# A decode kernel on one core: the last section of TensorE in another order, with products of zeros in its waits

## The chip, the cores and the metric

The kernel runs on one core of a Trainium2 chip. The metric is the device time of one execution in microseconds (us); lower is better. Every execution is recorded with three things: its time, its span (from the first to the last instruction of the core) and the mean clock that TensorE was granted, as a share of full speed. A full trace, with every instruction and transfer, is kept for one execution of each run. Nearly all runs below are of the state "fast"; a run with a single execution ("a look") has the state "unknown", and its span is then compared with the spans of fast executions.

## The reference, cut to what matters

One decoding step of four sequences: cached attention with 16 query heads on 8 key/value heads of 8192 positions, an output projection, and a small MLP that gates it.

```python
# x: (4, 1, 448); k_cache, v_cache: (4, 8, 8192, 256), bf16
xn = _layernorm(x)
q = (xn @ wq) ...                                  # 16 heads of 256
scores = einsum("bhqd,bhkd->bhqk", q, k) * 256 ** -0.5
o = einsum("bhqk,bhkd->bhqd", softmax(scores), v)
s = o.reshape(4, 1, 4096) @ wo                     # wo: (4096, 448)
g = silu(_B_ref(xn, w1, w2, w3, w4))               # MLP, short
return x + s * g
```

There are 32 pairs of sequence and key/value head. Each has a key tile and a value tile of 4 MB, so 268 MB come from memory, once.

## The kernel before

One queue (SP) streams key and value tiles in turn. TensorE turns the keys (transposes), multiplies them with the queries, and multiplies the values of two pairs earlier with the exponentials. The last section, `finish()`, runs after the loop: the value products of the last two pairs, and the output projection. The last value tile comes in four pieces, and behind it come three late pieces of `wo`, so that only little work is left after the last landing.

```python
PIECES = (0, 32, 48, 56, NCH)       # pieces of the last value tile
LATE = ((0, 1), (2,), (3,))         # heads of wo that are loaded last
NWARM = 18                          # products of zeros before the loop
# ... cut ...
# SP queue, at its end
load_v(NH - 2)
load_v(NH - 1)                      # four pieces: dvl0 to dvl3
for i, hs in enumerate(LATE):       # three pieces: dwl0 to dwl2
    load_wo(hs[0], hs[-1] + 1, "dwl%d" % i)
# ... cut ...
# TensorE
def f_tr(dst, width, slot=0):       # "turned products": fp32, 2 columns
    for dh in range(NHALF):
        for i in range(CP):
            ins = pe.matmul(dst(dh)[:, 0:width], po[:, slot, i*DH+dh:(i+1)*DH:NHALF],
                            sel[:, i, 0:width], start=(i == 0), stop=(i == CP - 1))
    return ins

def f_st(h):
    take(pe, "a_exp")
    pe.matmul(psm[:, P+REP:P+2*REP], ones_f[:, :], rowsum[:, h % 2, :], start=True, stop=True)
    if h < NH - 1:
        take(pe, "v_po")
    ins = f_tr(ot_dst, REP)
    if h == NH - 1:
        take(pe, "v_po")
        ins = f_tr(lambda dh: ot_dst(dh, 1), REP, 1)
    ins.then_inc(S["p_m3"], 1)

def finish():
    f_bc(h)
    take(pe, "dwo", 16)
    pe.wait_ge(S["g_f"], 1)
    f_ou(range(NLATE, HQ - 3 * REP))        # 12 output products
    take(pe, "v_po")
    take(pe, "dv%d" % ((h - 1) % 2), 16)    # next-to-last value tile
    f_pv(h - 1, 0, NCH)                     # its 32 value products
    f_st(h)                                 # sum, 8 + 8 turned products
    take(pe, "dvl0", 16)
    pb = PIECES[NPIECE - ND]
    f_pv(h, 0, PIECES[1], pb, vl)           # piece one
    take(pe, "v_ot")
    f_ou(range(HQ - 3 * REP, HQ - REP)).then_inc(S["p_ou"], 1)
    # ... cut: pieces two to four, then:
    take(pe, "dwl0", 16)
    f_o(LATE[0])
    # ... cut ...
    for i in range(1, len(LATE)):
        take(pe, "dwl%d" % i, 16)
        ins = f_o(LATE[i], i == len(LATE) - 1)   # the very last: 8 products
    ins.then_inc(S["p_o"], 1)
```

After the last product DVE does two small steps (times the gate, plus x) and the result is stored.

## Time and profile before

| | before |
|---|---|
| time, median of 3 executions | 658.86 us (658.5 to 659.02) |
| the execution of the trace | time **660.08 us**, span 658.0 us |
| DMA rate over the span | 424 GB/s |

From the page of the kernel before: the span, the busy times, three rows of the 40 slices (each digit the tenths of a slice), and the transfer queue.

```profile
span 658.0 us, 22911 instructions
PE 555.3 (84%) x9959; PEld 475.0 (72%) x9959; DVE 276.3 (42%) x593; ACT 256.1 (39%) x364; POOL 13.4 (2%) x77
...
PEclk9797999897899888789987978998788898877996
DMA  8999999999999999999999999999999999999995
...
q1 hardware_dynamic: 12336, 278.99, 99.0%
```

The DMA row stands at 9 to the end: the kernel is bound by its stream of 279 MB. TensorE's 84% lies under it. Only what stands behind the stream's end can be shortened by work on TensorE, so the end must be read closely.

The timeline of the end of the kernel before. Columns: start in us, duration of the group, engine, line, operation, output<-inputs and shapes, number of instructions, and in brackets the idle time before it.

```profile
636.95 0.75 PE L674 MATMUL pst<-wo_sb,OT 128*32 128x448 bf16 x12
640.29 3.58 PE L642 MATMUL psv<-vb,pT 128*4 128x512 bf16 x32 [2.59 <-PEq L244]
643.81 0.59 PE L628 MATMUL psm<-rowsum,ones_f 128*128 128x2 f32 x2
644.26 3.55 PE L616 MATMUL psm<-sel,po 128*128 128x2 f32 x16
647.74 1.88 PE L642 MATMUL psv<-kn,pT 128*4 128x512 bf16 x16
...
653.31 0.56 PE L694 MATMUL pst<-pT,kn 128*128 128x32 bf16 x16
653.79 0.38 PE L684 MATMUL pst<-wo_sb,OT 128*32 128x112 bf16 x16
654.33 0.61 PE L684 MATMUL pst<-wo_sb,OT 128*32 128x112 bf16 x32 [0.16 <-PEq L244]
```

The landings are read from the transfer records of the same trace: next-to-last value tile 640.2 us, pieces of the last one 645.1, 647.6, 648.8 and 650.1, late pieces of wo 651.3, 651.8 and **652.37**. The last product ended at 654.94, so it was 2.58 us late. I call this distance, from the last landing to the end of the last product, the *lateness*.

The windows view of the same end. Columns: stretch and its length, then busy time of TensorE's products, weight loads, DVE, ACT and POOL (instructions in brackets), granted clock, share of DMA busy, GB/s.

```profile
635.30:638.70 3.40, 1.46 (x21) 0.60 (x15) 1.28 (x4) 0.70 (x4) 0.00 (x0) 1.00 1.01 434
638.80:642.20 3.40, 1.91 (x20) 0.69 (x24) 0.00 (x0) 0.00 (x0) 0.00 (x0) 0.50 0.98 419
642.20:645.60 3.40, 3.40 (x25) 2.07 (x17) 0.69 (x1) 0.00 (x0) 0.00 (x0) 0.50 0.94 392
645.60:649.00 3.40, 3.40 (x27) 2.52 (x30) 0.52 (x3) 0.00 (x0) 0.00 (x0) 0.50 1.01 403
649.00:652.40 3.40, 3.32 (x49) 1.37 (x41) 1.32 (x2) 0.00 (x0) 0.00 (x0) 0.50 0.59 218
```

After a stretch with 1.46 us of work the clock is halved, and stays so for four stretches of 3.41 us (638.79 to 652.45; the drop comes 1.09 us into the wait of 2.59 us). In the first of them TensorE is busy for 1.91 us, in the other three for 3.32 us or more. In this trace the recorded clock is always at 0.5 or 1.0, and all its changes lie multiples of 3.41 us apart. I call such a stretch of 3.41 us a *window*, and the time at which one begins its *edge*.

### The profile page before, as it was taken

The page shows a single profiled execution, that of the slowest core. Times are in us where ns is not written, and L with a number is a line of the kernel's source. Part 1 is how long each engine was busy: PE and PEld are TensorE (multiplying, and loading weights), DVE is VectorE, ACT ScalarE, POOL GpSimd, SP SyncE. Part 2 cuts the span into 40 slices and gives each one's busy share as a digit, 9 for nine tenths or more (in the row PEclk, how much of TensorE's full clock was granted, in tenths as well). Part 3 has the DMA queues.
Part 4 walks back from the last instruction along what each step waited for, and adds up shares of the span by engine and source line. Part 5 has one row for each costly group of instructions (what it writes and reads, how often), then busy time and mean ns, then how long its engine had stood idle before and what let it go on. Part 6 is the DMA issues. An engine that isn't in the chain of part 4 may idle for free. (4 is left out here: it accounts for less than half of the span.)

```text
span 658.0 us, 22911 instructions
## 1 busy us (share of the span) xinstructions
PE 555.3 (84%) x9959; PEld 475.0 (72%) x9959; DVE 276.3 (42%) x593; ACT 256.1 (39%) x364; POOL 13.4 (2%) x77
## 2 busy tenths in 40 slices
PE   1898997987888988888898878898888889888877
PEld 0487886876766887676797757778776678767755
DVE  7453554443443443344433434444343344434431
ACT  4153454442433444333444423444333344433430
POOL 2000000000000000000000000000000000000000
PEclk9797999897899888789987978998788898877996
DMA  8999999999999999999999999999999999999995
GB/s 359 439 416 422 437 426 436 430 430 432 428 436 428 434 430 438 428 432 432 428 432 430 430 432 434 430 438 428 432 430 430 432 432 428 432 438 428 436 420 225
DMA packets 12370, 279.13 MB, mean 424 GB/s; under 512 B 1221, under 2 KB 3273, under 8 KB 3785
## 3 DMA queue, kind: packets, MB, share of 16 engines
q1 hardware_dynamic: 12336, 278.99, 99.0%
q8 instruction: 7, 0.11, 0.1%
q14 instruction: 3, 0.02, 0.0%
q10 hardware_dynamic: 24, 0.01, 0.0%
HBM read 278.99 MB, written 0.00 MB: 424 GB/s over the span
## 5 line engine op out<-in xcount | busy, mean ns | idle before, releaser
L586 PE MATMUL pst<-ident_b,kn 128*128 128x128 bf16 x4096 | 346.4, 238 | 76.8 <-PEq L244 76.5
L294 ACT ACTIVATE kT<-pst 128x1024 bf16<-128x1024 bf16 x224 | 229.5, 1025 | 359.1 <-ACTq L244 358.1
L586 PEld LDWEIGHTS pst<-ident_b,kn 128*128 128x128 bf16 x4096 | 274.8, 108 | 82.4 <-issue 81.9
L292 DVE COPY kT<-pst 128x1024 bf16<-128x1024 bf16 x288 | 197.5, 691 | 263.3 <-DVEq L244 263.3
L598 PE MATMUL psc<-qc,kT 128*128 128x2 bf16 x4096 | 178.8, 164 | 2.4 <-issue 2.4
L598 PEld LDWEIGHTS psc<-qc,kT 128*128 128x128 bf16 x4096 | 157.9, 98 | 31.1 <-issue 30.8
L642 PE MATMUL psv<-vb,pT 128*4 128x512 bf16 x1056 | 87.3, 386 | 2.6 <-PEq L244 2.6
L616 PE MATMUL psm<-sel,po 128*128 128x2 f32 x272 | 38.2, 263 | 0.0
L616 PEld LDWEIGHTS psm<-sel,po 128*128 128x128 f32 x272 | 36.2, 204 | 0.0
L642 PEld LDWEIGHTS psv<-vb,pT 128*4 128x4 bf16 x1056 | 22.0, 83 | 18.7 <-issue 4.7
L452 DVE TENSOR_REDUCE rmax<-psc 128x2 f32<-128x128 f32 x32 | 9.3, 292 | 48.1 <-DVEq L244 48.1
L470 DVE COPY po<-psv 128x512 f32<-128x512 f32 x34 | 23.5, 692 | 7.8 <-DVEq L244 7.1
L457 DVE TENSOR_REDUCE gmax<-psm 2x1 f32<-2x128 f32 x32 | 8.9, 279 | 34.7 <-DVEq L244 34.7
L316 ACT ACTIVATE pT<-psc,negb 128x64 bf16<-128x64 f32 x66 | 20.7, 333 | 5.4 <-ACTq L244 5.4
L610 PEld LDWEIGHTS psm<-diag,ones_f 2*128 2x128 f32 x66 | 13.5, 253 | 6.4 <-issue 5.2
L279 POOL COPY qc<-qT 128x4 bf16<-128x4 bf16 x32 | 5.9, 186 | 586.6 <-DVEq L469 569.1
L610 PE MATMUL psm<-diag,ones_f 2*128 2x2 f32 x66 | 16.2, 313 | 1.1 <-PEq L244 0.9
L316 ACT ACTIVATION_READ_ACCUMULATOR pT<-psc,negb 128x1 f32 x66 | 13.6, 206 | 0.0
L606 PEld LDWEIGHTS psm<-ident_f,rmax 128*2 128x2 f32 x32 | 2.6, 80 | 14.0 <-issue 14.0
L628 PE MATMUL psm<-rowsum,ones_f 128*128 128x2 f32 x66 | 12.2, 254 | 0.0
L534 PE MATMUL pst<-ident_b,xn_b 4*128 4x4 bf16 x14 | 0.6, 161 | 13.6 <-DVE xn_b L365 8.9
L628 PEld LDWEIGHTS psm<-rowsum,ones_f 128*128 128x128 f32 x66 | 10.0, 192 | 0.9 <-issue 0.9
(97 smaller groups left out, 105.3 us busy)
## 6 DMA issues: line engine op xcount, KB each, us to landing
kn<-in_A_k_cache_dram SPq DMA_DIRECT2D x32, 4096.0 KB, 25.7
vb<-in_A_v_cache_dram SPq DMA_DIRECT2D x31, 4096.0 KB, 30.9
vb<-in_A_wq_dram SPq DMA_DIRECT2D x1, 3584.0 KB, 11.4
vb<-in_B_w_dram SPq DMA_DIRECT2D x2, 1568.0 KB, 16.3
wo_sb<-in_A_wo_dram SPq DMA_DIRECT2D x1, 2688.0 KB, 44.1
kn<-in_A_v_cache_dram SPq DMA_DIRECT2D x1, 2048.0 KB, 24.8
kn<-in_A_v_cache_dram SPq DMA_DIRECT2D x1, 1024.0 KB, 26.9
kn<-in_A_v_cache_dram SPq DMA_DIRECT2D x2, 512.0 KB, 28.1
```

Source lines behind the costliest of these rows:

```text
L292: engine.tensor_copy(dst, src).then_inc(S["v_ev"], 1)
L294: engine.activation(dst, src, ACT.Copy).then_inc(S["a_ev"], 1)
L316: ins = act.activation(pv_p[:, :, hh], sc[:, :, hh], ACT.Exp, bias=negb[:, s, hh:hh + 1], scale=SCALE, accum_out=rowsum[:, s, hh:hh + 1])
L452: v.tensor_reduce(rmax[:, :], psc[h % 2][:, 0:NCH * REP].rearrange("p (k h) -> p h k", h=REP), AX.X, ALU.max).then_inc(S["v_rmax"], 1)
L457: v.tensor_reduce(gmax[:, :], psm[0:REP, 0:P], AX.X, ALU.max).then_inc(S["v_s"], 1)
L470: v.tensor_copy(po[:, slot], psv[:, 0:CP * DH]).then_inc(S["v_po"], 1)
L586: ins = pe.transpose(dst[:, t * P:(t + 1) * P], kn[:, h % 2, GC * j + kl, half * P:(half + 1) * P], ident_b[:, :])
L598: ins = pe.matmul(psc[h % 2][:, kk * REP:(kk + 1) * REP], kT[:, j % RING, t * P:(t + 1) * P], qc[:, h % 2, half, :], start=(half == 0), st ...
L610: pe.matmul(psm[:, P:P + REP], ones_f[0:REP, :], diag[:, :], start=True, stop=True).then_inc(S["p_m2"], 1)
L616: ins = pe.matmul(dst(dh)[:, 0:width], po[:, slot, i * DH + dh:(i + 1) * DH:NHALF], sel[:, i, 0:width], start=(i == 0), stop=(i == CP - 1))
L628: pe.matmul(psm[:, P + REP:P + 2 * REP], ones_f[:, :], rowsum[:, h % 2, :], start=True, stop=True)
L642: ins = pe.matmul(psv[o:o + CP * REP, 0:CP * DH], pT[:, h % 2, kk * REP:(kk + CP) * REP], src[:, kk:kk + CP, :].rearrange("p c d -> p (c d)"),
```

## The change

The intent: use the wait for the next-to-last value tile for work that doesn't need it (the sum of the last tile, the first half of the turned products), and fill waits with products of zeros, so that the clock is not halved. The turned products get a semaphore of their own for each half.

```diff
-    NWARM = 18
+    NWARM = 14
...
             f_negb(h)
-            f_po(h - 1, 1)
             take(v, "p_m3")
             f_ot(h - 2, True)
+            v.reciprocal(rz[:, h % 2, :], psm[:, P + REP:P + 2 * REP]).then_inc(S["v_s"], 1)
+            take(v, "v_s")
+            v.sem_inc(S["v_ot"], 1)
+            f_po(h - 1, 1)
+            take(v, "p_tr")
             f_ot(h - 1, True, 1)
             v.sem_inc(S["v_ot"], 1)
-            v.reciprocal(rz[:, h % 2, :], psm[:, P + REP:P + 2 * REP]).then_inc(S["v_s"], 1)
-            take(v, "v_s")
             take(v, "p_ou")
...
+            def f_warm(n):
+                for i in range(n):
+                    pe.matmul(psc[1 - h % 2][0:PVW, 0:D], pT[:, h % 2, NCH * REP:NCH * REP + PVW],
+                              wo_sb[:, NLATE, 0, :], start=True, stop=True)
...  (in finish)
                 take(pe, "v_po")
+                f_warm(4)
+                take(pe, "a_exp")
+                pe.matmul(psm[:, P + REP:P + 2 * REP], ones_f[:, :], rowsum[:, h % 2, :],
+                          start=True, stop=True)
+                f_tr(ot_dst, REP).then_inc(S["p_m3"], 1)
+                f_warm(2)
                 take(pe, "dv%d" % ((h - 1) % 2), 16)
                 f_pv(h - 1, 0, NCH)
-                f_st(h)
+                take(pe, "v_ot")
+                f_ou(range(HQ - 3 * REP, HQ - 2 * REP))
+                f_warm(2)
+                take(pe, "v_po")
+                f_tr(lambda dh: ot_dst(dh, 1), REP, 1).then_inc(S["p_tr"], 1)
+                f_warm(3)
                 take(pe, "dvl0", 16)
                 pb = PIECES[NPIECE - ND]
                 f_pv(h, 0, PIECES[1], pb, vl)
                 take(pe, "v_ot")
-                f_ou(range(HQ - 3 * REP, HQ - REP)).then_inc(S["p_ou"], 1)
+                f_ou(range(HQ - 2 * REP, HQ - REP)).then_inc(S["p_ou"], 1)
+                f_warm(3)
...
-                with nc.Fori(0, NH // 4, engines=[e], head_slot={e: 104}):
+                with nc.Fori(0, NH // 4, engines=[e], head_slot={e: 88}):
```

Cut: the declaration of the semaphore `p_tr`, and the simplified `f_st`, which now serves the loop only. The weights of a zero product are 32 columns of `pT` that stay zero; the place of the loop in the program moves by 16 slots.

More of the change, by code (lines that the diff above doesn't have):

```diff
@@ L156, in bass_recurrent_scan__gqa_block_cached__mixer_s_mlp__decode_kernel @@
             + ["dvl%d" % i for i in range(NPIECE)] + ["dwl%d" % i for i in range(len(LATE))]
-            + ["p_td", "p_ta", "p_sc", "p_m1", "p_m2", "p_m3", "p_ou", "p_pv", "p_x", "p_q", "p_h", "p_h2", "p_o"]
+            + ["p_td", "p_ta", "p_sc", "p_m1", "p_m2", "p_m3", "p_tr", "p_ou", "p_pv", "p_x", "p_q", "p_h", "p_h2", "p_o"]
             + ["v_ev", "a_ev", "v_rmax", "v_diag", "v_neg", "v_ot", "a_exp", "g_q", "g_c",
@@ L629, in f_st @@
                           start=True, stop=True)
-                if h < NH - 1:
-                    take(pe, "v_po")
-                ins = f_tr(ot_dst, REP)
-                if h == NH - 1:
-                    take(pe, "v_po")
-                    ins = f_tr(lambda dh: ot_dst(dh, 1), REP, 1)
-                ins.then_inc(S["p_m3"], 1)
+                take(pe, "v_po")
+                f_tr(ot_dst, REP).then_inc(S["p_m3"], 1)
             def f_pv(h, lo, hi, end=NCH, src=None):
@@ L705, in finish @@
                 take(pe, "v_po")
+                f_warm(4)
+                take(pe, "a_exp")
+                pe.matmul(psm[:, P + REP:P + 2 * REP], ones_f[:, :], rowsum[:, h % 2, :],
+                          start=True, stop=True)
+                f_tr(ot_dst, REP).then_inc(S["p_m3"], 1)
+                f_warm(2)
                 take(pe, "dv%d" % ((h - 1) % 2), 16)
                 f_pv(h - 1, 0, NCH)
-                f_st(h)
+                take(pe, "v_ot")
+                f_ou(range(HQ - 3 * REP, HQ - 2 * REP))
+                f_warm(2)
+                take(pe, "v_po")
+                f_tr(lambda dh: ot_dst(dh, 1), REP, 1).then_inc(S["p_tr"], 1)
+                f_warm(3)
                 take(pe, "dvl0", 16)
```

## The prediction

> **What bounds the kernel now.** DMA: the page gives the transfer queue 99.0% of 16 engines' span, and the 40 slices show the DMA row at 9 until the last. Only what stands after the last landing can be shortened on the compute side. From the trace's transfer records, the last landings are: next-to-last value tile 640.2 us; four pieces of the last value tile 645.1, 647.6, 648.8, 650.1; three late pieces of wo 651.3, 651.8, 652.4. In the timeline the last product ends at 654.95, two DVE steps end at 655.58, the span at 658.0. Of the 5.7 us tail some 3.4 us (8 products, two DVE steps of 0.28 us, 2.5 us of store) can't be avoided; 2.2 us is TensorE being late.
>
> **Why it is late.** After 12 output products (0.75 us) TensorE waits 2.59 us for the value tile (waits view; 637.70 to 640.29). The windows view shows the granted clock at 0.50 from 638.8 to 652.4. [...] At half clock 32 value products take 3.58 us, 16 turned fp32 products 3.55 us (8 take 1.08 us at full clock in the loop). Piece one's product starts at 647.74 (landed 645.1), the last piece's at 653.31 (landed 650.1).
>
> **What the change does.**
> - Removed: 4 of 18 zero products before the loop (0.2 us each); TensorE waits for the first key tile there anyway: 0.
> - Moved: sum of the last tile and 8 turned products (1.1 us at full clock) into the 2.59 us wait; four output products (0.2 us) and the other 8 turned products to between the value products and the landing at 645.1.
> - Added: 14 zero products of 448 columns, estimated 0.19 us each at full clock, 2.6 us of TensorE, nearly all in waits. The loop's place in the program moves by 16 slots; DMA limits the loop: 0.
>
> **Estimated course.** [...] Then: value products 640.3 to 642.1 (half of 3.58), second turned products done 644.0, piece one 645.1 to 646.0, piece two 648.0, last piece 650.7, and TensorE waits for each piece of wo. Last product 652.7, DVE 653.4, span 655.8: minus 2.2 us. All of it is critical, but the wo landing at 652.4 caps it: 0.35%.
>
> **Predicted time: 656.7 us**, 8 in 10 between 656.1 and 657.9. Faster by over 2%: 0.005; within 2%: 0.985; slower by over 2%: 0.01.
>
> **What would show it right.** Granted clock 1.0 (at most one half-clock window) from 635 to 652; next-to-last tile's value products in 1.8 us; turned products in two groups of 1.1 us; TensorE idle before the late wo products, the last ending 0.3 us after the landing; DMA rate unchanged.
>
> **What would make it wrong.** (a) The clock drops all the same[...]: then zero products cost twice and the gain shrinks to 1 us, or none. [...] (c) The wo landing is later. (d) A new hand-over with DVE costs more than the overlap gives.

Four passages are cut from the prediction, because they rest on statements about the clock and the loading of instructions that were not read from a trace of this case. That four zero products in the window before the drop are enough to keep the clock is only the author's estimate; no basis for it is shown. 2.2 us of lateness off the median of 658.86 us gives the 656.7 us. The times of a zero product can be worked out from the trace of before: those before the loop, of 512 columns, start 0.22 us apart at full clock and 0.43 us at half clock, so one of 448 columns takes about 0.19 us at full clock, which the trace after then shows (0.19 us apart). After the 18 of them TensorE stood idle for 0.32 us before its first product on a key tile.

## The result, and the profile after

| | before | after |
|---|---|---|
| time, median of 4 executions each | 658.94 us (658.5 to 659.2) | 658.34 us (658.18 to 658.84) |
| span of the traced execution | 658.0 us | 656.0 us |
| its time | 660.08 us | 658.18 us |

The ratio is 0.9993, with a 95% interval of 0.9976 to 1.001: the same. (Ratios are the mean time of one kernel's fast runs over that of the other's of the same rounds, so not quite the ratio of the medians.) The two traces differ by 2.0 us of span, nearly as predicted; the times differ by 0.6 us. The time was predicted at 656.7 us with a range to 657.9, and 658.34 lies outside.

The page of the changed kernel:

```profile
span 656.0 us, 22934 instructions
PE 554.9 (85%) x9969; PEld 475.1 (72%) x9969; DVE 276.4 (42%) x593; ACT 256.2 (39%) x364; POOL 13.4 (2%) x77
...
PEclk9698999887899888789987888988778987888998
DMA  8999999999999999999999999999999999999996
...
q1 hardware_dynamic: 12336, 278.99, 99.3%
```

Its timeline of the end (L668 are the zero products):

```profile
638.51 0.75 PE L677 MATMUL pst<-wo_sb,OT 128*32 128x448 bf16 x12
639.09 0.92 PE L668 MATMUL psc<-wo_sb,pT 128*32 128x448 bf16 x4
639.94 0.38 PE L711 MATMUL psm<-rowsum,ones_f 128*128 128x2 f32 x2
640.18 1.08 PE L618 MATMUL psm<-sel,po 128*128 128x2 f32 x8
...
641.20 0.39 PE L639 MATMUL psv<-vb,pT 128*4 128x512 bf16 x3
...
641.42 1.84 PE L639 MATMUL psv<-vb,pT 128*4 128x512 bf16 x28
...
644.58 1.07 PE L618 MATMUL psm<-sel,po 128*128 128x2 f32 x8 [0.54 <-PEq L244]
...
651.41 0.93 PE L687 MATMUL pst<-wo_sb,OT 128*32 128x112 bf16 x40 [0.45 <-PEq L244]
652.51 0.38 PE L687 MATMUL pst<-wo_sb,OT 128*32 128x112 bf16 x8 [0.17 <-PEq L244]
```

And the windows view, along the edges of this execution's clock:

```profile
638.10:641.40 3.30, 3.17 (x33) 2.26 (x37) 0.78 (x2) 0.70 (x4) 0.00 (x0) 1.00 0.92 392
641.50:644.80 3.30, 2.76 (x42) 1.51 (x34) 0.95 (x3) 0.00 (x0) 0.00 (x0) 1.00 0.95 402
644.90:648.20 3.30, 3.30 (x41) 1.81 (x40) 0.80 (x2) 0.00 (x0) 0.00 (x0) 1.00 0.99 398
648.30:651.60 3.30, 2.58 (x68) 2.29 (x68) 0.87 (x2) 0.00 (x0) 0.00 (x0) 1.00 0.80 298
```

The clock holds until 651.7 us, the turned products come as two groups of about 1.1 us, and TensorE now waits for wo: the last landing is at 652.38 (before: 652.37), the last product ends at 652.89, 0.51 us late. So in these two executions all went as foreseen. What does not fit is the times. The four executions of the changed kernel have spans of 656.0, 656.7, 656.2 and 656.1 us, each 2.14 to 2.20 us under its time. With about the same difference (2.08 us in its traced execution) the other executions of the kernel before, at 658.5 to 659.2 us, would have spans of about 656.4 to 657.1 us, and not 658.0.

### The profile page after: what moved, and what is told of

Read it like the earlier page. It is cut to its first block, busy times and chain, and to the rows that moved or that the text cites. A ratio compares the mean times of both kernels' runs of the same rounds, so it can differ in the third digit from the quotient of the medians.

```text
span 656.0 us, 22934 instructions
## 1 busy us (share of the span) xinstructions
PE 554.9 (85%) x9969; PEld 475.1 (72%) x9969; DVE 276.4 (42%) x593; ACT 256.2 (39%) x364; POOL 13.4 (2%) x77
## 5 line engine op out<-in xcount | busy, mean ns | idle before, releaser
L618 PE MATMUL psm<-sel,po 128*128 128x2 f32 x272 | 36.8, 257 | 0.5 <-PEq L244 0.5
L618 PEld LDWEIGHTS psm<-sel,po 128*128 128x128 f32 x272 | 34.7, 196 | 0.9 <-issue 0.9
```

What stands on the lines that cost most here:

```text
L618: ins = pe.matmul(dst(dh)[:, 0:width], po[:, slot, i * DH + dh:(i + 1) * DH:NHALF], sel[:, i, 0:width], start=(i == 0), stop=(i == CP - 1))
```

## The experiments

Theory A: the traced execution of before was one of its slow ones. Where the half clock falls in the last 20 us differs from execution to execution, and with it the lateness. Theory B: before always has a span of 658.0, and the changed kernel pays more outside its span. Theory C, a rival on the cause of the lateness: it does not go with the clock.

### First set: the two kernels again, and each half of the change alone

**The kernel before, unchanged**, five rounds.

> The kernel before, unchanged, to get the span of several of its executions beside their times. Theory A (the phase of the clock's windows): the one profiled execution of before, 658.0 us of span and 660.08 us of time, was a slow one; its other executions have spans of about 656.4 to 657.2, time minus span is 2.1 to 2.2 us as with the changed kernel, and where half clock falls in the last 20 us differs from execution to execution. Theory B (cost outside the span): every execution of before has a span near 658.0 and a time of only 658.9, so time minus span is about 0.9 us, and the changed kernel pays 1.3 us more outside its span (a longer program).

Measured: median 658.21 us (six executions, 657.69 to 660.79), spans 655.7, 656.1, 658.7, 656.0, 656.2 and 656.2 us. The eleven executions of before that ran beside it as the yardstick have spans of 656.1 to 657.6. Time minus span is 2.04 us in the mean. Theory A stands and B falls. The trace is of the execution with 655.7 us, which is *less* than the changed kernel's. Its last landing was at 652.14 and its last product 0.42 us late, with the same program as the one that was 2.58 us late:

```profile
638.06 0.75 PE L674 MATMUL pst<-wo_sb,OT 128*32 128x448 bf16 x12
640.05 3.26 PE L642 MATMUL psv<-vb,pT 128*4 128x512 bf16 x32 [1.24 <-PEq L244]
643.24 0.38 PE L628 MATMUL psm<-rowsum,ones_f 128*128 128x2 f32 x2
643.49 2.02 PE L616 MATMUL psm<-sel,po 128*128 128x2 f32 x16
```

The turned products take 2.02 us instead of 3.55. The windows view of the same execution shows why:

```profile
639.40:642.80 3.40, 2.75 (x28) 0.97 (x32) 0.00 (x0) 0.00 (x0) 0.00 (x0) 0.51 0.97 414
642.90:646.20 3.30, 3.30 (x42) 2.48 (x34) 1.04 (x3) 0.00 (x0) 0.00 (x0) 1.00 0.98 407
646.30:649.60 3.30, 3.20 (x45) 1.13 (x41) 1.49 (x3) 0.00 (x0) 0.00 (x0) 0.50 1.01 393
```

Here the edge of the clock's window fell 0.65 us later (639.44 in place of 638.79), and the value tile landed 0.25 us sooner (639.91 in place of 640.16). The window then held 28 value products in place of 20, and the full clock came back at 642.86. In the first trace it came back at 652.45.

**The changed kernel, unchanged**, five rounds, on the same chip.

> The changed kernel, unchanged, on the same chip. Theory A: time minus span 2.1 to 2.2 us, spans 656.0 to 656.7, 0.3 to 0.9 us under those of before in the mean. Theory B: the same spans, but before's are at 658.0, with times only 0.6 us apart.

Measured: median 658.56 us (658.19 to 658.68), mean span 656.26 us, where the yardstick's mean is 656.89. In time the means are 658.46 and 658.93: 0.47 us. The six executions of the kernel before that stand in the run above, on the same chip, have a mean span of 656.48 us, a mean time of 658.54 us and a median of 658.21 us, which is under the changed kernel's. With them counted as well, the differences shrink to 0.49 us of span and 0.33 us of time. The ratio is 0.9995 (0.9982 to 1.0008), the same. Time minus span is 2.20 us. In its trace the half clock begins at 651.9 and the lateness is 0.51 us, as in its first trace.

**The new order without the zero products.**

```diff
             def f_warm(n):
-                for i in range(n):
+                for i in range(0):
```

> The changed kernel with its 14 zero products in the last section left out; the new order stays. Theory A: the half clock comes in some executions, so the spans scatter as those of before do, but the order has moved 2 us of work into a wait and part of the gain stays: 0 to 0.5 us slower than the changed kernel. If the zero products were the whole gain: as before, 0.5 to 0.7 us over the changed kernel.

Measured: median 658.67 us, ratio 1.0 (0.9987 to 1.0012). In its trace the half clock came at 650.9 only, and the lateness is 0.51 us. One lucky trace can't tell anything in this kernel, as before's own had just shown, so it was looked at again in the third set.

**The zero products without the new order.** The kernel before, with NWARM = 14 and head_slot 88 as in the changed one, and:

```diff
                 take(pe, "v_po")
+                f_warm(6)
                 take(pe, "dv%d" % ((h - 1) % 2), 16)
                 f_pv(h - 1, 0, NCH)
+                f_warm(2)
                 f_st(h)
+                f_warm(3)
                 take(pe, "dvl0", 16)
...
                 f_ou(range(HQ - 3 * REP, HQ - REP)).then_inc(S["p_ou"], 1)
+                f_warm(3)
```

> The old order with 14 zero products at the matching places (6 before the wait for the next-to-last value tile, 2 after its products, 3 before the last tile's first piece, 3 before its second). Theory A: the clock holds in nearly all executions, spans 656.0 to 656.7 as the changed kernel's, within 0.3 us of it, so the zero products are what counts. If the order counts: 0.4 us or more over the changed kernel.

Measured: median 658.66 us, mean 658.53 us, which is 0.07 us over the changed kernel's mean, ratio 0.9996 (0.9983 to 1.0009). In its trace the clock is full from 634 to 655 us, and the lateness is 0.42 us. So the zero products alone can do what the trace after shows.

### Second set: does the lateness go with the clock?

Three looks at the unchanged kernel before:

> One more trace of the kernel before, unchanged. Theory A: how late the last product is after the last landing (2.6 us in the first trace, 0.4 us in the second) goes with where the clock's window edges fall between 638 and 642 us: late, 1 us or more, where the tail stays at half clock for three windows or more on end; 0.4 to 0.6 us where it is at half clock for two windows or fewer. Rival C: the lateness has another cause (landings of the values, DVE), and does not go with the half clock. The last landing of wo is at 652.1 to 652.8 in every trace.

> As the look before it: lateness goes with the number of half-clock windows on end in the tail (A), or does not (C).

> As the look before it: lateness goes with the number of half-clock windows on end in the tail (A), or does not (C).

And the kernel before with a semaphore that nothing uses, since time minus span was 0.14 us more in the kernels with the new semaphore:

```diff
-  "p_m3", "p_ou", ...
+  "p_m3", "p_tr", "p_ou", ...
```

> The kernel before with one semaphore more, that nothing uses. The time lay 2.17 to 2.20 us over the span in the 14 executions of the two kernels with the new semaphore, 2.04 to 2.05 us in those without it. If the semaphore costs that: 2.17 to 2.20 us here, with spans as those of before (655.7 to 658.7). If the new order or the hand-over costs it: 2.05 us here. It is one more trace of before's tail also, for theories A and C.

The unused semaphore costs nothing: time minus span 2.01 us (four executions), spans 656.4 to 657.1. That guess falls. Its trace counts as one more of before. The six traces together:

| trace of before | value wait, us | half clock between 638 us and the last landing | last landing | lateness |
|---|---|---|---|---|
| first | 2.59 | 638.8 to 652.4 | 652.37 | 2.58 |
| e1_before_again | 1.24 | 639.4 to 642.9, 646.3 to 649.7 | 652.14 | 0.42 |
| e2_look1 | 0 | 644.4 to the end | 652.44 | 1.16 |
| e2_look2 | 0 | 647.9 to the end | 652.71 | 1.18 |
| e2_look3 | 1.15 | 645.6 to 649.0, and from 652.4 | 653.29 | 0.51 |
| e2_before_sem | 1.15 | 645.6 to 649.0, and from 652.4 | 653.34 | 0.51 |

The lateness goes with the half clock near the end: 1.2 us where it lasts through the work after 650 us, 2.6 us where it lasts all through, 0.4 to 0.5 us where the clock is back by 650. Theory A holds, though not in the words in which I put it: what matters is less the number of half-clock windows on end than whether the last 3 us before the landing are among them (e2_look2 has only one whole window and is 1.18 us late). The mean lateness of the six is 1.06 us, not 2.58. One point was outside what I expected: the last landing itself moves from 652.1 to 653.3 us, by more than the whole gain of the change.

The look e2_look1 also shows that a high busy share alone does not keep the clock. Its windows view:

```profile
641.00:644.40 3.40, 3.40 (x42) 2.57 (x34) 0.69 (x1) 0.00 (x0) 0.00 (x0) 1.00 0.96 405
644.50:647.80 3.30, 2.53 (x28) 0.79 (x32) 0.52 (x3) 0.00 (x0) 0.00 (x0) 0.50 0.99 405
647.90:651.20 3.30, 3.26 (x39) 2.08 (x31) 1.31 (x2) 0.00 (x0) 0.00 (x0) 0.50 0.90 338
```

From 641.0 to 644.4 TensorE is busy for 3.40 of 3.40 us, and the clock is halved after it. In the changed kernel the stretch 641.5 to 644.8 holds 2.76 us, and the clock stays. In the first, 2.0 us are fp32 turned products of 2 columns, beside 20 value products; in the second, 26 value products of 512 columns, four output products and two zero products of 448, with only the start of a group of turned products. The number of columns does not settle it either. In a stretch of the loop in the first trace (256.5 to 259.9 us), 24 transposes of 128 columns stood beside 10 fp32 and 32 bf16 products of 2 columns, far fewer columns in all than the 20 value products of e2_look1 have, and the granted clock was 1.00 in it and in the stretch after it. What decides whether the clock is halved is not shown here.

### Third set: what the new order does

**The changed kernel without its new semaphore**, the second half of the turned products using the first half's.

```diff
-                f_tr(lambda dh: ot_dst(dh, 1), REP, 1).then_inc(S["p_tr"], 1)
+                f_tr(lambda dh: ot_dst(dh, 1), REP, 1).then_inc(S["p_m3"], 1)
...
-            take(v, "p_tr")
+            take(v, "p_m3")
```

> The changed kernel without the new semaphore: the second group of turned products uses the first group's semaphore, and DVE takes it twice. The unused semaphore cost nothing in the kernel before (time minus span 2.01 us), so time minus span should stay at 2.17 to 2.20 us if the new order costs it, and fall to 2.05 us if the semaphore costs it only where it is used. Spans as the changed kernel's, 656.0 to 656.7; last product 0.4 to 0.5 us after the last landing.

Measured: median 658.52 us, spans 656.0 to 656.6, time minus span 2.18 us. So the 0.14 us outside the span go with the new order and not with the semaphore. In the trace the clock is full until 654.7, and yet the lateness is 0.87 us, more than expected. Its timeline:

```profile
639.72 0.75 PE L677 MATMUL pst<-wo_sb,OT 128*32 128x448 bf16 x12
640.29 0.92 PE L668 MATMUL psc<-wo_sb,pT 128*32 128x448 bf16 x4
...
641.39 1.08 PE L618 MATMUL psm<-sel,po 128*128 128x2 f32 x8
...
642.41 0.38 PE L639 MATMUL psv<-vb,pT 128*4 128x512 bf16 x3
...
642.62 1.84 PE L639 MATMUL psv<-vb,pT 128*4 128x512 bf16 x28
```

In this execution TensorE came to the last section at 639.72. The value products, whose tile had long landed, then had to stand behind the zero products and the turned products until 642.4. In e2_look1, the old order with the same arrival (639.72), they start at 640.36. A late arrival alone does not make the 0.87 us, though: e1_order_only, the new order without zeros, came at 639.77 and was 0.51 us late, behind a last landing at 652.67 in place of 652.38.

**The same with two zero products more**, before the wait for the first late piece of wo.

> The same with two zero products more, before the wait for the first late piece of wo. In both traces of the changed kernel the clock fell to half at 651.7 to 651.9, so the last product ended 0.51 us after the last landing, where the old order with zero products had 0.42. If that is all that is left: 0.42 here and 0.1 us less in the mean, which five rounds will hardly tell; nothing more can come of TensorE, for the rest is landing, DVE steps and store.

Measured: median 658.25 us, ratio 0.9999 (0.9987 to 1.0011); five executions of 658.11 to 658.28 and one of 659.97. In the trace the clock is full to the end of the work and the lateness is 0.42 us, as expected.

**Two more looks at the new order without zero products.**

> Another trace of the new order without zero products, since its first one may have had lucky window edges (no half clock before 650.9, last product 0.51 us late). If the zero products hold the clock: half-clock windows between 638 and 650 in one or both of these two looks. Even then the new order should be 0.4 to 0.8 us late at most, since it does 1.1 us of turned products before the value tile lands.

> As the look before it: half-clock windows between 638 and 650 in one or both of the two looks if the zero products hold the clock, and the last product 0.4 to 0.8 us after the last landing even then.

Measured: spans 656.9 and 656.9 us, lateness 1.18 us in both, with the half clock from 646.6 and from 647.6 to the end. That is more than the 0.4 to 0.8 us expected: the order alone is as late as before is in its looks. The windows view of the first:

```profile
643.20:646.50 3.30, 2.24 (x32) 1.45 (x28) 0.87 (x2) 0.00 (x0) 0.00 (x0) 1.00 0.96 400
646.60:649.90 3.30, 2.03 (x36) 1.01 (x32) 1.26 (x2) 0.00 (x0) 0.00 (x0) 0.50 1.02 393
650.00:653.30 3.30, 3.20 (x60) 3.01 (x64) 0.18 (x1) 0.00 (x0) 0.00 (x0) 0.50 0.29 109
```

### Fourth set: is the new order needed once the zeros are there?

**The old order with 16 zero products**: the kernel with the zeros alone, and `f_warm(2)` before the wait for the first late piece of wo. This was the version that I hoped would beat both kernels.

> The old order with the 14 zero products and two more before the wait for the first late piece of wo. If the zero products are the whole gain: no half clock between 638 and 652, last product 0.42 us after the last landing, time minus span 2.05 us as before, so 658.0 to 658.4 us where the landing comes at 652.4, 0.3 us or more under the mean of before. If the new order is needed: last product 0.8 us late or more.

Measured: it does not beat them. The median is 658.91 us and the ratio 1.0014 (0.9999 to 1.0029), the same, because its six executions fall into two groups: 657.81, 657.91 and 657.93 us, and 659.89, 659.95 and 661.2 us. The trace is of one of the first group (lateness 0.42 us, landing 652.23). To catch one of the long ones, it was looked at twice more:

> One more trace of the old order with 16 zero products, to catch one of its long executions. If the span is 657.5 us or more: the transfer stream is the cause if the last landing is at 654 us or later with the last product 0.4 to 0.9 us after it; the clock is the cause if the landing is at 652 to 653 us and the product 1.5 us late or more. If the span is under 656.5: as its first trace, 0.42 us late, no news.

> As the look before it: a span of 657.5 us or more is the transfer stream's if the last landing is at 654 us or later, the clock's if the last product is 1.5 us late or more; a span under 656.5 us is no news.

Both were short (spans 656.4 and 656.0 us, lateness 0.67 and 0.42 us), so no long execution was traced. They occur in the kernel before also (660.79 and 659.98 us), and with the new order (659.97 us). What makes them long stays open.

**A second look at the old order with 14 zero products, and two more at the changed kernel.**

> A second trace of the old order with 14 zero products. If the zero products are the whole gain: no half clock between 638 and 650 and the last product 0.42 to 0.51 us after the last landing, as in the first trace. If that trace was luck: half clock and about 1.2 us.

> One more trace of the changed kernel. No half clock between 638 and 650. If the new order costs where TensorE comes late to the last section: the last product is 0.5 us late where the section's first product starts at 638.5 or sooner, and 0.8 to 0.9 us late where it starts at 639.7 or later, as in the kernel with one semaphore fewer.

> As the look before it: no half clock between 638 and 650; 0.5 us late where the last section's first product starts at 638.5 or sooner, 0.8 to 0.9 us where it starts at 639.7 or later, if the new order costs there.

Measured: the zeros alone have one half-clock window this time (644.9 to 648.3) and a lateness of 0.67 us, between the two cases expected. The changed kernel has 0.48 and 0.42 us, with half clock from 652.6. In both looks it came to the last section early, at 638.2 to 638.5, so they confirm one side of what I expected of late arrivals; the other side rests on the one trace above, of the kernel with one semaphore fewer.

All traces by kernel:

| kernel | traces | lateness, us | half clock before 650 us |
|---|---|---|---|
| before (one with an unused semaphore) | 6 | 2.58, 1.18, 1.16, 0.51, 0.51, 0.42; mean 1.06 | in 6 |
| new order alone | 3 | 1.18, 1.18, 0.51; mean 0.96 | in 2 |
| old order with 14 or 16 zeros | 5 | 0.67, 0.67, 0.42, 0.42, 0.42; mean 0.52 | in 2, one window each |
| new order with 14 or 16 zeros | 6 | 0.87, 0.51, 0.51, 0.48, 0.42, 0.42; mean 0.54 | in 0 |

So the traces show no need of the new order once the zeros are there: the mean lateness is 0.52 us without it and 0.54 us with it.

All executions with a recorded span:

| kernel | executions | median time | mean time | time minus span |
|---|---|---|---|---|
| before | 50 | 658.68 us | 658.66 us | 2.04 us |
| the changed kernel | 11 | 658.30 us | 658.37 us | 2.19 us |
| new order alone | 7 | 659.03 us | 658.85 us | 2.18 us |
| old order, 14 zeros | 6 | 658.49 us | 658.48 us | 2.05 us |

These pool several sets on at least five chips and the looks, and leave out the first trace of before, so they are a picture.

## Why the prediction was right or wrong

**Right: what bounds the kernel.** The stream ran at 424 and 426 GB/s, its last landing came at 652.37 and 652.38 us in the two first traces, and the work of the loop was not touched.

**Right: the mechanism.** Half clock made TensorE late (32 value products took 3.58 us at it in the trace of before, and 1.90 us at full clock in e2_look1), and zero products help to keep the clock. In all six traces with the new order and zeros it held to 651.7 us at least; in two of three traces of the same order without them it did not. They are no guarantee: in two of five traces of the old order with zeros one window was at half clock. And that four of them are enough in the window before the drop was an estimate; how many are needed was not tested by any run. The turned products took 1.08 and 1.07 us (predicted: two groups of 1.1), the span of the trace was 656.0 us (predicted: 655.8). That the two first traces also differ by nearly the predicted 2.2 us is luck of the execution that was traced: set against the trace e1_before_again (span 655.7 us), the changed kernel would have lost 0.3 us.

**Wrong: the size, in one term of the sum.** The step that failed reads: "Of the 5.7 us tail some 3.4 us [...] can't be avoided; 2.2 us is TensorE being late", and then "span 655.8: minus 2.2 us", set against the median of the timed executions (658.86 − 2.2 gives the 656.7). The 2.2 us were read from one execution, the slowest that was then known: it took 660.08 us when the others took 658.5 to 659.0. The loss that was read from it was not in the median from which it was subtracted. Six traces have a mean lateness of 1.06 us where that one has 2.58; the four of the changed kernel have 0.48. The term measures 1.06 − 0.48 = 0.58 us in these traces, and not 2.2. It is no settled figure: the six values run from 0.42 to 2.58 us, and without the first trace the mean of before is 0.76 us and the term 0.28. The mean spans give 0.63 us for the yardstick of the first set (656.89 − 656.26), 0.49 with the six other executions of before on that chip, and 0.44 over all executions of the last table (656.626 − 656.182).

The data to see it were at hand. Time and span of the traced execution gave time minus span, 2.08 us. The predicted span of 655.8 plus 2.08 is 657.9 us, 1.2 us over the 656.7 that I wrote. The prediction named a drop of the clock as a danger for the changed kernel, and did not ask whether the drop in the trace of before comes at the same time in every execution. It does not: in the six traces of before the first half clock after 638 us begins at 638.8, 639.4, 644.4, 645.6, 645.6 and 647.9 us.

**Wrong: the wait that was to be filled.** "TensorE waits 2.59 us for the value tile" held for that execution only; in the other five it was 1.24, 1.15, 1.15, 0 and 0 us. The moved products therefore often do not fill a wait but stand before the value products, which start at 641.2 us in the first trace after (predicted 640.3) and at 642.4 us in the trace with a late arrival. The order alone gains nothing that the runs show (mean lateness 0.96 us against 1.06); its two late traces (1.18 us) had the half clock through the last landing.

**Not foreseen: 0.14 us outside the span.** Every kernel with the new order has a time minus span of 2.18 to 2.19 us, every one with the old order 2.01 to 2.05 us. It is not the semaphore. What it is was not found. The balance: 0.58 us less lateness, 0.14 us more outside the span, so about 0.44 us. The runs show 0.47 us between the changed kernel and the yardstick of the first set, 0.33 us when the six other executions of before are counted in, and 0.29 us between all executions; they agree no closer than that. The last landing of before alone scatters by 1.2 us in its six traces (652.14 to 653.34); that of the changed kernel lay between 652.17 and 652.41 in four.

**Left open:** the rare long executions, the 0.14 us, and the scatter of the last landing.

## What to carry to other kernels

Before a loss read in one trace is subtracted from a median, compare the time of the traced execution with that of the others: if it is longer by about the loss, the loss is in that execution, not in the median. Where the granted clock is halved at other times from execution to execution (here first between 638.8 and 647.9 us in six traces of one kernel, with a lateness of 0.42 to 2.58 us), one trace of a tail is one draw, and several looks are needed to know what is usual. A stretch in which TensorE is busy throughout can still be followed by half clock (3.40 of 3.40 us in e2_look1), so the granted clock is to be read and not inferred from the busy share; and work moved ahead of a wait gains only if the wait is there in most executions.
